# Adaptive-norm attention and gated feed-forward on one core: a prologue rearranged around a half-size scale block, and the output weights loaded by rows of 128 partitions

## The chip, the cores and the metric

One NeuronCore of a Trainium2 chip runs the whole block. The metric is the device time of one execution in microseconds (us). Durations of single instructions come from one profiled execution.

## The reference, cut to what matters

```
mod = (silu(c) @ w_mod).reshape(1, 6, 1, 1024)      # c: 1x1024, w_mod: 1024x6144
sa, ca, ga, sb, cb, gb = mod[:, 0..5]
h = layernorm(x) * (1 + ca) + sa                    # x: 2048x1024
q, k, v = split(h @ wqkv, 32 heads of 32)
pq, pk = phi(q), phi(k)     # phi(t) = (t + 1 if t > 0 else exp(t)) + 1e-6
kv = sum over tokens of pk^T v;   z = sum over tokens of pk
o = (pq @ kv) / (pq . z + 1e-6)                     # per head
x = x + ga * (o @ wo)
h = layernorm(x) * (1 + cb) + sb
x = x + gb * ((silu(h @ w_gate) * (h @ w_up)) @ w_down)   # 3584 wide
```

All inputs and the output are bf16.

## The kernel before, in words

The 2048 tokens are four blocks (`sc`, 0 to 3) of 512, each four tiles of 128. Attention needs kv and z over all tokens first: so for each block the program does K, then V (block 0: V, then K, then Q), and kv of the block before inside the next block's K. Then come Q of the other blocks, the output projection (`wo_tile`), and the feed-forward (`gate_up`, `down`), which is most of the time. A K, V or Q group is eight matmuls of 128x128x512 into one of four PSUM banks (`acc_a`, pool `pa`); other sums take a second pool of four (`acc_b`).

**What sets the order.** `mm` and `transpose` (L97, L100) keep TensorE in program order. `in_order` (L83) does the same for VectorE, ScalarE and GpSimd in the prologue (L474 to L529). Elsewhere the scheduler places instructions when it thinks them ready, by program order among ready ones; `tc.issue_after(x)` holds one back until `x`. All loads but two go through SP's queue. `hold_back` (L369) writes one element of a tile that a load will fill, after the latest phi, so that the load cannot start before that point.

**The prologue.** `c` is turned onto partitions by a small matmul and silu gives `scT`. `w_mod`'s columns 1024 to 2047 (`ca`, tiles `wca`, 2 MB) are loaded first, then `wv` with x tiles 2 and 3 between, `sa`'s block `wsa` and `wk`. `mod_rows(1, ...)` (L255) makes the `ca` row from `wca` with matmuls of 256 columns on four column groups, `mod_turn` (L262) turns it onto partitions. `hT` holds block 0's normalised tokens turned by TensorE (`pe_transpose_tile`, L217), `hs` the same times (1 + ca). V of block 0 uses `hs`, since the shift by `sa` is added to V's sums later; `mod_rows(0, ...)` makes `sa` during V, `modulate_all` (L413) then applies both to `hT` for K and Q. `sc_row`, silu(c) along the free axis on all partitions, comes from eight small matmuls (L485 to L489). `keep_warm` matmuls on zeros (`sel`) fill TensorE's waits.

**The other four rows of `mod`.** `mod_load(q, cols)` (L374) loads one row's block of `w_mod` turned, by two DMA transposes into two tiles of 4x1024; each `mod_step` (L384) multiplies one 128x1024 row set by `sc_row` on VectorE and sums it into one column. Row 2 (`ga`) is loaded at the end of block 0, row 3 in block 1, row 4 in block 3. `K_STEPS` and `V_STEPS` (L400) say how many steps go where. `ga_spread` (L403) brings `ga` along the free axis to all partitions by way of DRAM.

**wo.** In block 2, after the fourth K group, `wo` is loaded into two tiles [128, 4, 1024] (L550 to L556): eight DMAs, each to 32 partitions with four rows of 1024 on each. `wo_v` (L62) is `"(h g i e) n -> h g e i n"`. In block 3 each row is multiplied by `ga` on VectorE (L568 to L572). `ln1(sc)` (L242) gives block `sc` its `hT`: statistics, `xn` on ScalarE, and one DMA transpose per tile on SP (L239), then the modulation on VectorE. That of block 3 is made during block 2's late K groups and V.

**The fold.** After the last kv, `fold_wo(h, nb)` (L602) multiplies kv into `wo`: 16 matmuls of 32x32x512, each on a tile of the array of its own, into four `acc_b` banks, copied back over `wo` by ScalarE and VectorE. Four of these stand between Q groups.

Of the kernel before, what the change touches and what calls it, by code (L numbers as in the profile page):

```python
# [21 lines left out]
def kernel(  # L22
# [13 lines left out]
    nc = tc.nc  # L36
# [77 lines left out]
    c_sb = const.tile([DC, P], BF16, name="c_sb")  # L114

# [8 lines left out]
    for st in range(2):  # L124
        load_x(st, nc.sync)
# [3 lines left out]
    wca = [big("wme", [4, D]) for _ in range(2)]  # L129
# [6 lines left out]
    for j in range(DC):  # L136
        load_block(wca, wm_v, j, D, nc.scalar if j == 0 else nc.sync)
    for cc in range(DC):
        load_block(wv, wqkv_v, cc, 2 * D)
        if cc in (1, 4):  # L140
            load_x(2 + cc // 4, nc.sync)
# [26 lines left out]
    sc_row = const.tile([P, D], BF16, name="sc_row")  # L168
# [11 lines left out]
    sel = const.tile([P, HPC, P], BF16, name="sel")  # L180
# [17 lines left out]
    def bn(src, mv_out):  # L198
        stats = small.tile([P, NNB, nc.vector.BN_STATS_DIM], F32, name="stats")
        for i in range(NNB):  # L200
            nc.vector.bn_stats(out=stats[:, i, :], in_=src[:, i * NB:(i + 1) * NB])  # L201
        nc.vector.bn_aggr(out=mv_out, in_=stats[:])

    def normalise(dst, src, mean, rstd):
        nc.vector.tensor_scalar(out=dst, in0=src, scalar1=mean, scalar2=rstd, op0=ALU.subtract, op1=ALU.mult)

    def normalise_act(dst, src, mv, rstd):
        nmr = small.tile([P, 1], F32, name="nmr")
        last_nmr[0] = nc.gpsimd.tensor_scalar(out=nmr[:], in0=mv[:, 0, 0:1], scalar1=rstd[:, 0:1], scalar2=-1.0,  # L209
                                op0=ALU.mult, op1=ALU.mult)  # L210
        nc.scalar.activation(out=dst, in_=src, func=ACT.Identity, bias=nmr[:], scale=rstd[:, 0:1])  # L211
# [5 lines left out]
    def pe_transpose_tile(hT, xn, t):  # L217
        tp = acc_b("tp", (DC, P), BF16)
        for cc in range(DC):
            transpose(tp[:, cc, :], xn[:, cc * P:(cc + 1) * P])  # L220
        nc.vector.tensor_copy(out=hT[:, :, t * P:(t + 1) * P], in_=tp[:])
# [3 lines left out]
    def ln1_stats(sc, t):  # L225
        x_sb = x_tiles.pop(sc * STC + t)
        mv = small.tile([P, STC, 2], F32, name="mv")
        bn(x_sb, mv[:, 0, :])
        rstd = rstd_of(mv, 1)
        return sc, t, x_sb, mv, rstd  # L230

    def ln1_norm(sc, t, x_sb, mv, rstd, dve=False):
        xn = k2.tile([P, D], BF16, name="xn", bufs=4)
        if dve:
            normalise(xn[:], x_sb[:], mv[:, 0, 0:1], rstd[:, 0:1])
        else:
            normalise_act(xn[:], x_sb[:], mv, rstd)
        if sc > 0:
            last_load[0] = nc.sync.dma_start_transpose(hTs[sc][:, :, t * P:(t + 1) * P], xn[:])  # L239
        return xn  # L240
# [14 lines left out]
    def mod_rows(q, lo, hi, first=None):  # L255
        for j in range(lo, hi):
            if first is not None:
                mm(first, lhsT=wca[j // 4][:, j % 4, 0:P], rhs=scT[:, j:j + 1], start=False, stop=j == DC - 1)
            row_matvec(mod_ps[:, q * MW:(q + 1) * MW], sc32[:, j, :], (wsa, wca)[q][j // 4][:, j % 4, :],
                       q == 0 and j == 0, j == DC - 1)  # L260
# [4 lines left out]
    def scale_to(hs, hT, cc, lo, hi):  # L265
        nc.vector.tensor_scalar(out=hs[:, cc, lo:hi], in0=hT[:, cc, lo:hi], scalar1=ca0T[:, cc:cc + 1], scalar2=None,
                                op0=ALU.mult)

# [105 lines left out]
    def mod_load(q, cols, held=False):  # L374
        ts = [big("wmt", [DC // 2, D]) for _ in range(2)]
        if held:
            hold_back(ts)
        for h, t in enumerate(ts):
            lo = q * D + h * NB
            last = nc.sync.dma_start_transpose(t[:], w_mod[:, lo:lo + NB])  # L380
            mod_steps.extend((t[:, i, :], cols[:, 4 * h + i:4 * h + i + 1]) for i in range(DC // 2))
        return last
# [71 lines left out]
    nc.vector.memset(sel[:], 0.0)  # L454

    def keep_warm(acc, n):
        for _ in range(n):
            mm(acc[:], lhsT=sel[:, 0, :], rhs=sel[:], start=True, stop=True)

    def keep_warm_f32(acc, n):  # L460
        zeros = sel[:].rearrange("p h n -> p (h n)").bitcast(F32)
        for _ in range(n):
            mm(acc[:, 0:zeros.shape[1]], lhsT=zeros[:, 0:P], rhs=zeros, start=True, stop=True)

    accs = [acc_a() for _ in range(4)]
    spare = accs[3]
    keep_warm_f32(spare, 3)
    keep_warm(spare, 1)
# [5 lines left out]
    with in_order(nc.vector, nc.scalar, nc.gpsimd):  # L474
        mod_ps = acc_b("mod_ps")
        mm(mod_ps[:, 0:DC], lhsT=c_sb[:], rhs=ident[0:DC, 0:DC], start=True, stop=True)
        for g in range(4):
            mm(mod_ps[g * DH:(g + 1) * DH, MW:2 * MW], lhsT=ident[:, 0:DH], rhs=base_t[:, 0:MW], start=True, stop=False)
        nc.scalar.activation(out=scT[:], in_=mod_ps[:, 0:DC], func=ACT.Silu)
        xn0 = ln1_norm(*ln1_stats(0, 0))  # L480
        st1 = ln1_stats(0, 1)
        nc.vector.tensor_copy(out=sc32[:], in_=scT[:].unsqueeze(2).to_broadcast([P, DC, DH]))
        xn1 = ln1_norm(*st1, dve=True)
        keep_warm_f32(spare, 1)
        for h in range(2):  # L485
            for j in range(DC // 2):
                mm(accs[h][:, j * P:(j + 1) * P], lhsT=scT[:, 4 * h + j:4 * h + j + 1].to_broadcast([P, P]), rhs=ident[:],
                   start=True, stop=True)
            nc.scalar.copy(out=sc_row[:, h * NB:(h + 1) * NB], in_=accs[h][:])  # L489
        keep_warm(spare, 3)  # L490
        first = accs[2][:, 0:1]
        mm(first, lhsT=ident[:], rhs=base_t[:, 0:1], start=True, stop=False)
        mod_rows(1, 0, 3, first)
        pe_transpose_tile(hT, xn0, 0)
        pe_transpose_tile(hT, xn1, 1)
        mod_rows(1, 3, DC, first)
        keep_warm(spare, 1)
        nc.vector.tensor_scalar(out=hs[:, 0, 0:H], in0=hT[:, 0, 0:H], scalar1=first, scalar2=None, op0=ALU.mult)
        mod_turn(DC, 2 * DC)
        for cc in range(1, 4):  # L500
            scale_to(hs, hT, cc, 0, H)
        xn2 = ln1_norm(*ln1_stats(0, 2))
        for cc in range(4, DC):
            scale_to(hs, hT, cc, 0, H)
        st3 = ln1_stats(0, 3)
        gs = k_groups[0:4]
        v_mms(hs, gs, accs, 0, 6)
        pe_transpose_tile(hT, xn2, 2)
        for cc in range(DC):
            scale_to(hs, hT, cc, H, H + P)  # L510
        xn3 = ln1_norm(*st3)
        v_mms(hs, gs, accs, 6, DC)
        gs2, accs2 = k_groups[4:6], [acc_b("acc") for _ in range(2)]
        v_mms(hs, gs2[0:1], accs2[0:1])
        v_evac(0, gs, accs)
        pe_transpose_tile(hT, xn3, 3)
        for cc in range(DC):
            scale_to(hs, hT, cc, H + P, SCW)
        v_mms(hs, gs2[1:2], accs2[1:2])
        mod_rows(0, 0, DC)  # L520
        mod_turn(0, DC)
        nc.vector.tensor_copy(out=sca[:], in_=scr[:, :, :, 0])
        v_evac(0, gs2, accs2)
        for g in k_groups[6:8]:
            acc = acc_a()
            v_mms(hs, [g], [acc])
            v_evac(0, [g], [acc])
        modulate_all(hT, ca1T, saT)
# [4 lines left out]
    for h in range(2):  # L533
        with tc.issue_after(last_load[0].ins):
            nc.sync.dma_start(out=wq[h][:], in_=wqkv_v[:, 4 * h:4 * h + 4, 0:D])
# [5 lines left out]
    for sc in range(NSC):  # L541
        if sc > 0:
            k_phase(sc, 0, 2)
            kv_phase(sc - 1)
            k_phase(sc, 2, 3)
            if sc == 1:
                mod_load(3, sbT, True)
                mod_step(1)
            k_phase(sc, 3, 4)
            if sc == 2:  # L550
                wo = [big("wo", [4, D]) for _ in range(2)]
                hold_back(wo)
                for h in range(2):
                    for g in range(4):
                        with tc.issue_after(last_load[0].ins):
                            last_load[0] = nc.sync.dma_start(out=wo[h][g * DH:(g + 1) * DH, :, :], in_=wo_v[h, g])  # L556
            if sc == 3:
                mod_load(4, cbT, True)
            k_phase(sc, 4, 8)
        if sc == 0:  # L560
            k_phase(0, 0, 8)
# [24 lines left out]
        if sc == 0:  # L586
            with tc.issue_after(last_load[0].ins):
                last_load[0] = mod_load(2, gaT)

    q_phase(1, 0, 1, 2)  # L590
    q_phase(1, 1, 2)
# [10 lines left out]
    def fold_wo(h, nb):  # L602
        ns = slice(nb * NB, (nb + 1) * NB)
        ps = [acc_b("wf") for _ in range(4)]
        for i in range(HPC):
            for g in range(4):
                rs = slice(g * DH, (g + 1) * DH)
                mm(ps[g][i * DH:(i + 1) * DH, :], lhsT=KVT[rs, h, i * DH:(i + 1) * DH], rhs=wo[h][rs, i, ns],
                   start=True, stop=True)
        for g in range(4):  # L610
            (nc.scalar.copy if g % 2 == 0 else nc.vector.tensor_copy)(out=wo[h][:, g, ns], in_=ps[g][:])

    q_phase(1, 2, 5)
# [5 lines left out]
    den_sum(0, acc_a())  # L619
    fold_wo(0, 0)  # L620
    den_spread(0)
    q_phase(1, 6, 8)
    fold_wo(0, 1)
    q_phase(2, 0, 2)
    fold_wo(1, 0)
    q_phase(2, 2, 4)
    fold_wo(1, 1)
# [3 lines left out]
    def wo_tile(st):  # L631
# [10 lines left out]
        for nb in range(NNB):  # L642
            ns = slice(nb * NB, (nb + 1) * NB)
            a_ps = acc_b("a_ps")
            for hg in range(HG):
                mm(a_ps[:], lhsT=pq[:, hg, t * P:(t + 1) * P], rhs=wo[hg // 4][:, hg % 4, ns],
# [145 lines left out]
```

## Time and profile before

| | us |
|---|---|
| median of 3 runs | 829.96 (829.62 to 830.33) |
| the profiled execution | 830.19 |
| its span, first to last instruction | 828.4 |
| first V matmul (block 0) starts | 11.13 |
| first K matmul (block 0) starts | 27.60 |
| wo's loads issued | 94.7 to 97.9 |
| first K matmul of block 3 starts | 113.00 |
| the four folds start | 155.1, 159.1, 163.0, 166.9 |

A page of a profile gives busy time by engine, a picture of the span in 40 slices, DMA queues, the chain of work that ended last, and the costliest groups of instructions. PE is TensorE, DVE VectorE, ACT ScalarE, POOL GpSimd, SP SyncE; a q after an engine is its queue of DMA issues. In a group's line, `a<-b` is output and inputs by the program's names, and what follows is partitions x elements. A timeline's columns are start, duration, engine, line, operation and count. A window's columns are the stretch, its length, busy time and count of instructions of PE, PEld (weight loads), DVE, ACT and POOL, the granted clock, the busy share of the 16 DMA engines (which can pass 1, since packets overlap) and GB/s.

### The profile page before, as it was taken

How to read it: one execution, taken by the hardware profiler on the slowest of the kernel's cores; microseconds unless marked ns; L12 is line 12 of the kernel's file. 1: busy time of each engine (PE TensorE's matmuls, PEld its weight loads, DVE VectorE, ACT ScalarE, POOL GpSimd, SP SyncE). 2: the span in 40 equal slices, each digit the busy share in tenths (PEclk: the TensorE clock that was granted, in tenths of full speed). 3: DMA queues.
4: the chain of work that ended last, by engine and by line, in shares of the span. 5: the costliest groups of instructions: out<-in, count | busy, mean ns of one | idle time of the engine just before them, and what ended most of it. 6: DMA issues, size and time to landing. Idle time of an engine off the chain costs nothing.

```text
span 828.4 us, 11209 instructions
## 1 busy us (share of the span) xinstructions
PE 818.2 (99%) x4531; PEld 379.1 (46%) x4609; DVE 348.7 (42%) x680; ACT 168.1 (20%) x253; POOL 64.0 (8%) x165
## 2 busy tenths in 40 slices
PE   8999999999999999999999999999999999999998
PEld 4444444444444444444444444444444444444444
DVE  6868778886353344422222354222224432222222
ACT  3535343434111101101111010111111101111000
POOL 2101020120222002000000010000001100000000
PEclk9999999999999999999999999999999999999999
DMA  9968444139995836456342262753405529610011
GB/s 347 301 167 187 124 112 102 41 96 320 368 246 196 251 110 181 150 168 195 103 158 96 62 222 88 254 187 110 145 0 182 149 65 358 217 47 1 19 58 51
DMA packets 142212, 129.07 MB, mean 156 GB/s; under 512 B 58768, under 2 KB 120720, under 8 KB 141648
## 3 DMA queue, kind: packets, MB, share of 16 engines
q1 hardware_dynamic: 138208, 115.10, 46.3%
q0 software_dynamic: 3792, 12.98, 5.0%
q8 instruction: 36, 0.59, 0.3%
q10 hardware_dynamic: 160, 0.26, 0.1%
q14 instruction: 16, 0.13, 0.0%
HBM read 101.98 MB, written 12.72 MB: 138 GB/s over the span
## 4 chain that ended last, share of the span: by engine, by line
PE 97%; DMA 2%; issue 1%; DVE 0%; ACTq 0%; SPq 0%
PE acc L98 89%; PE a_ps L98 7%; DMA wv<-in_A_wqkv_dram 1%; PE kvp L98 1%; DMA wme<-in_w_mod_dram 0%; PE wf L98 0%; PE den L98 0%; PE mod_ps L98 0%; PE vb L98 0%; ACTq L126 0%; PE tp L101 0%; SPq L134 0%; DVE e L708 0%; DVE ob L711 0%
## 5 line engine op out<-in xcount | busy, mean ns | idle before, releaser
L98 PE MATMUL acc<-h2T,wgu 128*128 128x512 bf16 x1755 | 385.6, 379 | 1.9
L98 PEld LDWEIGHTS <-wgu 128*128 128x128 bf16 x1792 | 175.3, 98 | 211.3
L687 DVE TENSOR_TENSOR gu<-acc,e 128x512 bf16<-128x512 f32 x112 | 77.5, 692 | 289.9 <-PE acc L98 278.8
L98 PE MATMUL acc<-wd,gu 128*128 128x512 bf16 (+2 forms) x908 | 195.2, 372 | 0.9
L686 ACT ACTIVATE e<-acc 128x512 f32<-128x512 f32 x112 | 66.9, 597 | 374.8 <-PE acc L98 363.4
L98 PEld LDWEIGHTS <-gu 128*128 128x128 bf16 x924 | 89.3, 98 | 104.5
L708 DVE TENSOR_TENSOR e<-acc,gb_bc 128x512 f32<-128x512 f32 (+2 forms) x33 | 22.3, 675 | 131.7 <-PE acc L98 122.8
L98 PEld LDWEIGHTS <-hT 128*128 128x128 bf16 x448 | 43.6, 98 | 52.3
L98 PE MATMUL a_ps<-wo,pq 128*128 128x512 bf16 x250 | 56.9, 379 | 0.3
L98 PE MATMUL acc<-hT,wq 128*128 128x512 bf16 x250 | 55.9, 379 | 0.6 <-issue 0.5
L98 PE MATMUL acc<-wk,hT 128*128 128x512 bf16 x252 | 55.9, 379 | 0.4 <-issue 0.3
L273 ACT ACTIVATE eb<-acc 128x512 bf16<-128x512 f32 x64 | 37.6, 594 | 61.7 <-PE acc L98 57.3
L211 ACT ACTIVATE xn<-x,nmr,rstd 128x1024 bf16<-128x1024 f32 x16 | 19.8, 1240 | 126.2 <-POOL nmr L209 125.4
L98 PE MATMUL acc<-wv,hT 128*128 128x512 bf16 x186 | 41.6, 379 | 0.3
L98 PEld LDWEIGHTS <-pq 128*128 128x128 bf16 x256 | 25.1, 98 | 30.2
L655 POOL DMA_DIRECT2D x_scratch<-x x16 | 9.8, 615 | 373.5 <-DVE x L648 373.4
L98 PEld LDWEIGHTS <-wq 128*128 128x128 bf16 x256 | 24.6, 98 | 29.9 <-issue 1.1
L274 DVE TENSOR_SCALAR eb<-eb 128x512 bf16<-128x512 bf16 x64 | 18.3, 290 | 26.0 <-ACT eb L273 26.0
L648 DVE TENSOR_TENSOR x<-a_ps,x_sb 128x512 f32<-128x512 f32 x32 | 22.1, 691 | 8.6 <-PE a_ps L98 7.9
L195 POOL TENSOR_TENSOR rstd<-veps,neg_half 128x1 f32<-128x1 f32 x32 | 18.0, 561 | 99.5 <-DVE veps L193 87.0
L201 DVE BATCH_NORM_STATS2 stats<-x_sb 128x6 f32<-128x512 bf16 x32 | 20.9, 674 | 4.4 <-DMA x_sb<-in_A_x_dram 4.3
L711 DVE TENSOR_TENSOR ob<-e,x1r 128x512 bf16<-128x512 f32 (+2 forms) x33 | 22.3, 675 | 1.0
(99 smaller groups left out, 320.6 us busy)
## 6 DMA issues: line engine op xcount, KB each, us to landing
wgu<-in_B_w_gate_dram SPq DMA_DIRECT2D x28, 1024.0 KB, 6.4
wgu<-in_B_w_up_dram SPq DMA_DIRECT2D x28, 1024.0 KB, 7.9
x_sb<-in_A_x_dram SPq DMA_DIRECT2D x32, 256.0 KB, 5.3
x_scratch<-x POOLq DMA_DIRECT2D x16, 512.0 KB, 3.1
x1r<-x_scratch SPq DMA_DIRECT2D x31, 256.0 KB, 2.9
wd<-in_B_w_down_dram SPq DMA_DIRECT2D x7, 1024.0 KB, 6.7
rbc<-rden_scratch POOLq DMA_DIRECT2D x16, 256.0 KB, 8.1
out_dram<-ob SPq DMA_DIRECT2D x31, 128.0 KB, 1.7
```

The lines of the kernel that those rows point to most:

```text
L98: return tc.keep_in_program_order(nc.tensor.matmul(out, lhsT=lhsT, rhs=rhs, start=start, stop=stop))
L195: nc.gpsimd.tensor_tensor(out=rstd[:, 0:n], in0=veps[:, 0:n], in1=neg_half[:].to_broadcast([P, n]), op=ALU.pow)
L201: nc.vector.bn_stats(out=stats[:, i, :], in_=src[:, i * NB:(i + 1) * NB])
L211: nc.scalar.activation(out=dst, in_=src, func=ACT.Identity, bias=nmr[:], scale=rstd[:, 0:1])
L273: nc.scalar.activation(out=e[:], in_=acc, func=ACT.Exp)
L274: nc.vector.tensor_scalar(out=e[:], in0=e[:], scalar1=1.0, scalar2=PHI_EPS, op0=ALU.min, op1=ALU.add)
L648: nc.vector.tensor_tensor(out=x1[:, ns], in0=a_ps[:], in1=x_t[:, ns], op=ALU.add)
L655: nc.gpsimd.dma_start(out=x1_dram[st * P:(st + 1) * P, :], in_=x1[:])
L686: nc.scalar.activation(out=sg[:], in_=ps[0][:], func=ACT.Silu)
L687: gm = nc.vector.tensor_tensor(out=guT[sc][f // GPT][:, f % GPT, :], in0=ps[1][:], in1=sg[:], op=ALU.mult)
L708: nc.vector.tensor_tensor(out=yt, in0=y_ps, in1=gb_bc[:, ns], op=ALU.mult)
L711: nc.vector.tensor_tensor(out=ob, in0=yt, in1=x1r, op=ALU.add)
```

## The change

- **Scale block in halves.** `wca` is loaded as two column halves of 512 (`load_ca`), each four DMAs of two row chunks. The first half comes ahead of `wv`'s first four chunks, the second ahead of x tile 3 and the other four. The first half's columns are made by matmuls of one column (`ca_cols`), and the first four chunks of `hs` are scaled straight from PSUM; the second half still goes through rows and a turn (`ca_rows`). V's groups run first on chunks 0 to 3, then on 4 to 7.
- **x tile 2 earlier**, ahead of the weights; tile 1's normalisation is split between VectorE and ScalarE; `hT` is copied from PSUM by ScalarE.
- **Two key groups side by side.** K's first two groups of block 0 take each chunk of `wk` in turn (`k_mms(0, k_groups[0:2], pair)`); the modulation of `hT` is done in two halves of 256 tokens. In later blocks kv stands after the first K group, not the second.
- **sc_row** is silu of one loaded row, written to DRAM by GpSimd and read back to all partitions by SP behind `wq`.
- **Turned `w_mod` loads half a block later.** Row 2's second half moves to block 1, row 3's second half to block 2, ahead of `wo`.
- **wo** is loaded by eight DMAs, each to 128 partitions with one row of 1024 on each.
- **The fold** writes into tiles of its own (`wof`) in three batches of 5, 6 and 5 units, each unit four matmuls and one copy, with one or two `acc_a` banks beside the `acc_b` ones.

```diff
-    wca = [big("wme", [4, D]) for _ in range(2)]
+    wca = [big("wme", [DC, NB]) for _ in range(2)]
...
-    for j in range(DC):
-        load_block(wca, wm_v, j, D, nc.scalar if j == 0 else nc.sync)
-    for cc in range(DC):
+    def load_ca(h, eng0):
+        for k in range(4):
+            js = slice(2 * k, 2 * k + 2)
+            (eng0 if k == 0 else nc.sync).dma_start(out=wca[h][:, js, :], in_=wm_v[:, js, D + h * NB:D + (h + 1) * NB])
+
+    load_ca(0, nc.scalar)
+    nc.scalar.dma_start(out=sc_row[0:1, :], in_=c)
+    for cc in range(4):
         load_block(wv, wqkv_v, cc, 2 * D)
-        if cc in (1, 4):
-            load_x(2 + cc // 4, nc.sync)
+    load_ca(1, nc.sync)
+    load_x(3, nc.sync)
+    for cc in range(4, DC):
+        load_block(wv, wqkv_v, cc, 2 * D)
...
+        def ca_cols(k):
+            for i in range(4):
+                for j in (2 * k, 2 * k + 1):
+                    mm(cols[i], lhsT=wca[0][:, j, i * P:(i + 1) * P], rhs=scT[:, j:j + 1], start=False,
+                       stop=j == DC - 1 and i in (0, 3))
...
+        v_mms(hs, gs, accs, 0, 1)
+        turn_half(xn1, 1, 1)
...
+        v_mms(hs, gs, accs, 1, 3)
+        tp2 = turn_tile(xn2)
...
+        v_mms(hs, gs, accs, 3, 4)
+        ca_rows()
+        mod_turn(DC + 4, 2 * DC)
...
+        gs2, accs2 = k_groups[4:6], [acc_b("acc") for _ in range(2)]
+        v_mms(hs, gs2, accs2, 0, 4)
...
+        v_mms(hs, gs, accs, 4, DC)
...
-            k_phase(sc, 0, 2)
+            k_phase(sc, 0, 1)
             kv_phase(sc - 1)
-            k_phase(sc, 2, 3)
+            k_phase(sc, 1, 3)
             if sc == 1:
-                mod_load(3, sbT, True)
+                mod_load(2, gaT, (1,), True)
+                mod_load(3, sbT, (0,), True)
                 mod_step(1)
             k_phase(sc, 3, 4)
             if sc == 2:
+                last_load[0] = mod_load(3, sbT, (1,), True)
                 wo = [big("wo", [4, D]) for _ in range(2)]
                 hold_back(wo)
                 for h in range(2):
-                    for g in range(4):
+                    for i in range(HPC):
                         with tc.issue_after(last_load[0].ins):
-                            last_load[0] = nc.sync.dma_start(out=wo[h][g * DH:(g + 1) * DH, :, :], in_=wo_v[h, g])
+                            last_load[0] = nc.sync.dma_start(out=wo[h][:, i, :], in_=wo_v[h, :, :, i, :])
...
+    wof = [big("wof", [4, D]) for _ in range(2)]
+    fold_units = [(h, nb, g) for h in range(2) for nb in range(NNB) for g in range(4)]
...
+    def fold_wo(accs):
+        units = [(fold_units.pop(0), acc) for acc in accs]
         for i in range(HPC):
-            for g in range(4):
+            for (h, nb, g), acc in units:
                 rs = slice(g * DH, (g + 1) * DH)
...
+    fold_wo([acc_b("wf") for _ in range(3)] + [acc_a() for _ in range(2)])
...
+    q_phase(2, 0, 1)
+    fold_wo([acc_b("wf") for _ in range(4)] + [acc_a() for _ in range(2)])
+    q_phase(2, 1, 4)
+    fold_wo([acc_b("wf") for _ in range(4)] + [acc_a()])
```

## The prediction, made before the changed kernel was run

> **What bounds the kernel now.** I read the page's first, second and fourth parts, then the chain of waits in order of time, then the timeline around every place that the diff touches.
>
> ```profile
> span 828.4 us, 11209 instructions
> ...
> PE 818.2 (99%) x4531; PEld 379.1 (46%) x4609; DVE 348.7 (42%) x680; ACT 168.1 (20%) x253; POOL 64.0 (8%) x165
> ...
> q10 hardware_dynamic: 160, 0.26, 0.1%
> ...
> PE 97%; DMA 2%; issue 1%; DVE 0%; ACTq 0%; SPq 0%
> ```
>
> TensorE is the chain. From 27.6 us to the end its matmuls of 512 columns start 0.216 us apart and no gap is over 0.6 us, so a change gains only ahead of 27.6 us or in instructions removed, and loses wherever it makes TensorE wait. The q10 line comes back below. The chain of waits shows the only DMA in it:
>
> ```profile
> 1.33 3.80 DMA wme<-in_w_mod_dram
> 5.52 5.48 DMA wv<-in_A_wqkv_dram
> 11.02 6.37 DMA wv<-in_A_wqkv_dram
> ```
>
> The first 11 us go to 2.5 MB of loads ahead of the first V matmul (11.13 us). The second place to look at is block 2, where `wo` is loaded and the transposes of the next block's `hT` follow on the same queue. SP's timeline there, one tile's view, and the matmuls and VectorE work after it:
>
> ```profile
> 94.66 3.65 SPq L556 DMA_DIRECT2D wo<-in_A_wo_dram  x8
> 101.72 7.08 SPq L239 DMA_TRANSPOSE hT<-xn  x4
> ```
> ```profile
> L556 SPq DMA_DIRECT2D wo<-in_A_wo_dram x8: 332/430/431, 94.7 to 97.9; - x8
> ...
> DMA to landing us min/median/max: 3.9/5.9/7.6
> ```
> ```profile
> 111.02 2.76 DVE L214 TENSOR_SCALAR hT<-hT,sca 128x512 bf16<-128x512 bf16 x8
> ```
> ```profile
> 113.00 3.62 PE L98 MATMUL acc<-wk,hT 128*128 128x512 bf16 x16
> ```
>
> The fourth transpose lands at 110.89 us (its completion count in the trace), the eight modulations run 111.02 to 113.78, and K of block 3 starts at 113.00. Its last chunk is needed at 113.00 + 7 x 0.216 = 114.5, so the slack of this chain is 0.7 us. What delays `hT` of block 3 by more stalls TensorE one for one; nothing stands ahead of K in its program order. Last, the DMA rate in two stretches of 2 us, the first in `wo`, the second in the prologue's 128-partition loads (last column GB/s):
>
> ```profile
> 102.00:104.00 2.00, 2.00 (x11) 0.94 (x10) 1.79 (x6) 2.00 (x4) 0.29 (x2) 1.00 1.07 246
> ```
> ```profile
> 18.00:20.00 2.00, 2.00 (x11) 0.88 (x9) 1.31 (x8) 2.00 (x4) 1.47 (x34) 1.00 1.05 390
> ```
>
> All 16 engines are busy in both. The packet records say why the rates differ: a 2,048-byte packet takes a median 84 ns in the prologue (10 to 20 us) and 155 ns in `wo` (95 to 104 us).
>
> [...] q10 carried the 8-row load of `c` and one 128-row load; 160 packets are 8 + 128 of data and 24 completion counts, 8 for the one and 16 for the other. So the 8-row load ran on 8 engines. [...] the first transpose was issued at 101.72, but its first 256-byte packet starts at 104.07, when the last `wo` packets are ending (104.9). [...]
>
> **The change part by part.**
>
> *wo loads (L552-556).* Removed: eight loads of 32 partitions x 4 rows. Added: eight of 128 partitions x 1 row, the same 2 MB and 1,024 packets. But the source view `wo_v[h, :, :, i, :]` has dimensions g (4, step 128 rows), e (32, step 1 row) and columns: g and e don't merge, so its slowest dimension is 4. [...] Four engines then carry 1,024 / 4 = 256 packets each, against 64 each on 16 before. Low bound of a packet: 84 ns, 21.5 us in all. High bound: 155 ns, 39.7 us[...]. I take 120 ns, the middle: 30.7 us.
>
> Timing: everything before is shifted by the prologue's gain, 1.2 us (below). Block 2's fourth K group is done at 93.2 (94.4 before). New there is one `w_mod` transpose (the half moved from block 1) ahead of `wo`: 4.2 us of SP time (that form's median issue). wo is issued from 97.5, its packets start 0.95 us later as before, behind the transpose's: 99.0. They end at 99 + 30.7 = 129.7. The four `hT` transposes queue behind on those four engines: 64 packets of 18 ns each per transpose and engine, 4.6 us; landing about 134.7; one modulation 0.35 and its start 0.15: K of block 3 at 135.2. It is planned for 113.0 - 1.2 = 111.8. **Stall 23.4 us** (14.2 at 84 ns, 32.7 at 155). What is moved past: the hT transposes, and three x loads (L636, not needed until about 172 us). SP's own eight-semaphore rotation (100 to 109 in the trace) makes the transposes wait for the first four `wo` loads as well, inside the same time.
>
> *Clock after the stall.* [...] I take 1.0.
>
> *Prologue.* Loads ahead of the first V matmul fall from 11 pieces of 256 KB to 8 (three of x, four of half a scale block, one of `wv`). Landings were 0.675 us apart: the 8th came at 8.75 us. The half-block pieces are 1 KB packets, 46 ns in the trace's `wgu` loads, against 42 per KB: four pieces cost 0.3 more, so `wv` lands near 9.05, and V starts near 9.2, 1.9 us earlier. Added on TensorE ahead of K: the second half's rows (32 matmuls of 128 columns, about 0.6), four more transposes (0.27), and a wait for that half, which lands near 14.3 while TensorE gets there at 13.5 (0.8). Taken away: stalls of about 0.5. V, 64 x 0.216 = 13.8, both late transposes 1.06, rows of `sa` 1.0, added in order, end at 26.4 against 27.6. VectorE has 8 us of work in that stretch of 16 and hides. Side by side, K's first two groups end at 26.4 + 3.45 = 29.85 against 31.05; `wk`'s last piece (28.68 before, 0.6 later now) lands at 29.3, used at 29.4. **-1.2** (between 0 and the DMA limit, -1.9).
>
> *Fold.* 64 matmuls of 32x32 in three batches instead of four. Before:
>
> ```profile
> L98 PE MATMUL wf<-wo,kvs x64: 384/384/385, 155.1 to 167.0; 32*32 32x512 bf16 x64
> ```
>
> Each batch of 16 uses 16 different tiles of the array, which start 3.4 ns apart: 0.46 us from the last wide matmul's end to the next one's start, 1.84 in four. Batches of 5, 6 and 5 units bring one row group twice, so every column step has two matmuls on one tile. If the queue stays in order behind the second, a batch takes 4 x 0.23 + 0.38 = 1.3, three 3.9: +2.1. If each tile waits alone, about 0.67 each: +0.2. I take **+2.0**[...]. Its five or six copies (0.59 and 0.68 us) lie beside 3.5 us or more of wide matmuls on two engines.
>
> *The rest at nothing.* kv one group earlier: v's last copy ends about 0.7 us after its matmuls, a K group covers 1.73. `sc_row` by way of DRAM: one 256 KB load behind `wq`, which lands near 38.3, needed at 40.2. `wof`: two tiles more while `wo` still lives, when `wv`, `wk` and v are dead.
>
> **Sum.** The profiled execution took 830.19, span 828.4 and 1.8 around it, 0.2 above the median of 829.96. -1.2 + 2.0 + 23.4 + 1.0 = +25.2, so about 855.
>
> **The rivals.** *R1: wo runs on 16 engines*[...]. For it: nothing in this trace shows a 4-row outer dimension. Against it: the 8-row load. Then wo takes 2 MB at 390 GB/s, 5.4 us, ends near 104.4, the transposes wait on their inputs as now, and K isn't late. Time 829.96 - 1.2 + 0.2 to 2.0: 829 to 831, **829.4 if the fold's tiles wait alone**, so not slower. It decides when wo ends before about 106.
> *R2: four engines, but the transposes reach the queue ahead of wo.* For it: the program orders SP by readiness, not by the text (an L636 load stands before wo now). Against it: the first transpose is ready 7 us after wo is. About 831.
> The ends of the forecast itself[...] are no rivals but its range.
>
> **How the numbers follow.** Forecast 0.75, its own range 844 to 865; R1 0.20; R2 0.05. A measurement here tells 0.2%, 1.7 us, from no change. Slower: 0.75, and 0.05 of the rivals where the fold costs its full price and the prologue gains little. Faster: 0.03 of R1. Same: 0.17. The range reaches to R1: 829 to 865.
>
> **What would show it.** Forecast right: wo's time to landing grows from 5.9 us towards 10 or more with about 60 GB/s moved, hT's four transposes land after 125 us, and TensorE has one gap of 14 to 33 us before K of block 3. First V matmul near 9.2, K near 26.4, each fold batch near 1.3 us. Wrong: no gap before that K, and wo's packets at 84 ns on all engines.

## The result, and the profile after

The change costs 2.5%: 850.8 us (median of 4 runs, 850.28 to 851.89) against 829.8 us for the kernel before (median of 4, 829.62 to 830.33), a ratio of 1.0254 with a 95% interval of 1.0236 to 1.0272. The prediction had about 855 and slower. The profiled execution took 851.21 us with a span of 849.4.

The page's first lines, and the group that carries block 3's first K matmul:

```profile
span 849.4 us, 11327 instructions
...
PE 827.4 (97%) x4623; PEld 380.1 (45%) x4623; DVE 346.4 (41%) x685; ACT 173.8 (20%) x261; POOL 65.3 (8%) x167
...
PEclk9999987999999999999999999999999999999999
...
L98 PE MATMUL acc<-wk,hT 128*128 128x512 bf16 x256 | 58.3, 387 | 17.3 <-DVE hT L224 17.2
```

TensorE is busy 9.2 us longer, the span is 21.0 longer: most of the loss is idle time. The last line says which: 17.2 us ahead of a K matmul, ended by VectorE's modulation of `hT`. The clock picture dips in slices 6 and 7 (106 to 149 us), so part of the longer busy time is slow time. TensorE and then VectorE there (start, duration, engine, line, operation, count, idle time before it and what ended it):

```profile
107.63 6.85 PE L98 MATMUL acc<-wv,hT 128*128 128x512 bf16 x31
131.71 3.59 PE L98 MATMUL acc<-wk,hT 128*128 128x512 bf16 x8 [17.23 <-DVE hT L224]
```
```profile
131.24 2.67 DVE L224 TENSOR_SCALAR hT<-hT,sca 128x512 bf16<-128x512 bf16 x8 [19.02 <-DMA hT<-xn]
```

VectorE had been waiting too, for a DMA, so the modulation is only the last link. SP's timeline shows the DMA's own queue, and two windows its rate (last two columns: busy share of the 16 engines, GB/s):

```profile
95.88 4.07 SPq L392 DMA_TRANSPOSE wmt<-in_w_mod_dram  x1
100.13 13.64 SPq L607 DMA_DIRECT2D wo<-in_A_wo_dram  x8
113.88 12.98 SPq L247 DMA_TRANSPOSE hT<-xn  x3
```
```profile
104.00:106.00 2.00, 2.00 (x11) 0.94 (x10) 1.93 (x8) 1.50 (x2) 0.91 (x3) 1.00 0.25 96
110.00:112.00 2.00, 2.00 (x11) 0.93 (x10) 2.00 (x3) 0.81 (x2) 0.00 (x0) 1.00 0.27 102
```

A busy share of 0.25 is that of four engines of 16 at work. In the trace each `wo` load has five completion counts (16 in the kernel before): one 0.4 us after the end of its issue and four later on, for the first load at 101.26 and at 105.89 to 106.61. Its 2,048-byte packets take a median 84 ns. They run from 101.6 to 125.6 us. The four transposes land at 126.6, 127.6, 128.7 and 131.1, and K of block 3 starts at 131.71.

The ledger, from the starts of the same matmuls in both traces:

| | before | after | what it adds |
|---|---|---|---|
| K of block 0 starts | 27.60 | 28.59 | +1.0 |
| K of block 2 starts | 84.11 | 85.44 | +0.3 |
| gap ahead of K of block 3 | none | 17.4 | +17.4 |
| from K of block 3 to the output projection's first matmul | 59.47 | 61.86 | +2.4: halved clock 2.2, fold 0.2 |
| the output projection's first matmul | 172.47 | 193.57 | sum +21.1 |

The clock record is halved from 119.5 to 136.6 us: the first eight K matmuls after the gap start 0.426 us apart, and kv takes 0.49 longer (8 x 0.21 + 0.49 = 2.2).

The prologue gained nothing. TensorE's first 12 us (`acc<-gb_bc` are the f32 matmuls on zeros of `keep_warm`, the one-column ones are `ca_cols`):

```profile
4.81 2.06 PE L98 MATMUL acc<-gb_bc 128*128 128x512 f32 x2
6.65 0.24 PE L98 MATMUL col<-scT,wme 128*128 128x1 bf16 x2
6.75 0.30 PE L98 MATMUL mod_ps<-scT,wme 128*128 128x1 bf16 x6
6.91 2.91 PE L98 MATMUL acc<-gb_bc 128*128 128x512 f32 x4
...
11.89 1.04 PE L98 MATMUL acc<-wv,hs 128*128 128x512 bf16 x4
```

The loads landed as predicted (`ca`'s half pieces at 6.5, 7.06, 7.75 and 8.46, the first of `wv` at 9.12), but V starts at 11.89. The second filler, four records, takes 2.91 us at the halved clock and stands in TensorE's program order ahead of the second pair of column chunks. The clock became full at 10.29; in the kernel before at 4.67.

The fold's first batch of five units (the last eight of its twenty matmuls, and the wide ones behind them; the group of five is one matmul at 176.12 and four from 176.28 on):

```profile
176.11 0.39 PE L98 MATMUL wf<-wo,kvs 32*32 32x512 bf16 x3
176.12 0.59 PE L98 MATMUL acc<-wo,kvs 32*32 32x512 bf16 x5
176.64 5.35 PE L98 MATMUL acc<-hT,wq 128*128 128x512 bf16 x24
```

### The profile page after: what moved, and what is told of

It is laid out like the page before. It is cut to its first block, busy times and chain, and to the rows that moved or that the text cites. A ratio compares the mean times of both kernels' runs of the same rounds, so it can differ in the third digit from the quotient of the medians.

```text
span 849.4 us, 11327 instructions
## 1 busy us (share of the span) xinstructions
PE 827.4 (97%) x4623; PEld 380.1 (45%) x4623; DVE 346.4 (41%) x685; ACT 173.8 (20%) x261; POOL 65.3 (8%) x167
## 4 chain that ended last, share of the span: by engine, by line
PE 97%; SPq 1%; DMA 0%; DVE 0%; issue 0%; ACT 0%; DVEq 0%
PE acc L98 89%; PE a_ps L98 7%; SPq L247 1%; PE kvp L98 1%; DMA hT<-xn 0%; PE mod_ps L98 0%; PE tp L101 0%; PE den L98 0%; PE wf L98 0%; PE vb L98 0%; ACT v L321 0%; SPq L691 0%; DVE gb_bc L466 0%; DVE hT L224 0%; DVE e L763 0%
## 5 line engine op out<-in xcount | busy, mean ns | idle before, releaser
L763 DVE TENSOR_TENSOR e<-acc,gb_bc 128x512 f32<-128x512 f32 (+2 forms) x33 | 22.3, 676 | 131.6 <-PE acc L98 128.7
L98 PE MATMUL acc<-wk,hT 128*128 128x512 bf16 x256 | 58.3, 387 | 17.3 <-DVE hT L224 17.2
L98 PE MATMUL a_ps<-wof,pq 128*128 128x512 bf16 x256 | 57.4, 379 | 0.0
L98 PEld LDWEIGHTS <-wq 128*128 128x128 bf16 x256 | 24.6, 98 | 30.7 <-issue 1.7
L221 ACT ACTIVATE xn<-x_sb,nmr,rstd 128x1024 bf16<-128x1024 bf16 (+1 forms) x17 | 19.6, 1163 | 14.3 <-POOL nmr L216 14.2
```

The lines of the kernel that those rows point to most:

```text
L98: return tc.keep_in_program_order(nc.tensor.matmul(out, lhsT=lhsT, rhs=rhs, start=start, stop=stop))
L221: nc.scalar.activation(out=dst[:, ws], in_=src[:, ws], func=ACT.Identity, bias=nmr[:], scale=rstd[:, 0:1])
L763: nc.vector.tensor_tensor(out=yt, in0=y_ps, in1=gb_bc[:, ns], op=ALU.mult)
```

## The experiments

The theory: `wo` on four engines, with `hT`'s transposes behind it on the same queue, makes the gap and the halved clock after it (19.6 of 21.1 us). The rival: the loss comes of the new order in block 2 (a turned `w_mod` load ahead of `wo`, kv one group earlier) or of the tiles of 128 partitions. The first four kernels separate these. Each experiment's kernel has its number; 1, 3 and 4 start from the changed kernel, 2 from the kernel before. Ratios are to runs of the kernel before that were made beside them: medians 829.97 us for 1 to 4, 830.14 for 5 to 8, 830.28 for 9 and 10.

**1. wo as before, the rest of the change kept.**

```diff
-                    for i in range(HPC):
+                    for g in range(4):
...
-                            last_load[0] = nc.sync.dma_start(out=wo[h][:, i, :], in_=wo_v[h, :, :, i, :])
+                            last_load[0] = nc.sync.dma_start(out=wo[h][g * DH:(g + 1) * DH, :, :], in_=wo_v[h, g])
```

> The changed kernel with wo loaded as before: eight transfers of 32 partitions. Theory (four engines for the wo loads): their 256 packets on each of four engines are gone, the loads take 9.3 us as before, starting behind the moved w_mod transpose at about 101.6 us and ending near 111; the four hT transposes end near 116, some 2 us after K of block 3 is due (114.3), so a stall of 2.4 us is left, no halved clock: 829.8 + 1.3 (prologue and up to block 3) + 2.4 + 0.1 = 833.6. Rival (the w_mod transpose moved ahead of wo causes the stall, and the shape of wo's loads does not matter): 849 to 851, as the changed kernel.

Measured 833.38 us, ratio to before 1.0046 (1.0029 to 1.0063). That undoes 17.4 of 21.0 us. What is left shows in TensorE's timeline:

```profile
113.87 2.65 PE L98 MATMUL acc<-wk,hT 128*128 128x512 bf16 x8 [1.53 <-DVE hT L224]
116.45 1.22 PE L98 MATMUL kvp<-v,pk 128*32 128x64 bf16 x128
117.83 0.81 PE L98 MATMUL acc<-wk,hT 128*128 128x512 bf16 x3 [0.16 <-issue]
119.63 2.75 PE L98 MATMUL acc<-wk,hT 128*128 128x512 bf16 x12 [0.98 <-issue]
```

K of block 3 still waits 1.5 us for `hT`, and its eight matmuls are paced by VectorE (0.323 us apart, not 0.216: 0.75 in all). The wait of about 1.1 us at 119.63, with no releaser, I had not expected; it comes back below. In this execution the clock was full at 5.71, V of block 0 began at 9.80 and K at 26.50, close to the 9.2 and 26.4 of the prediction.

**2. The wo loads alone, put into the kernel before.** The diff of 1 turned round, on L554 to L556.

> The kernel before with nothing changed but wo's loads: eight transfers of 128 partitions from a source whose outermost dimension is 4. Theory: wo runs on four engines from 95.6 us at 84 ns a packet, about 23 us, to 118.6; the hT transposes land near 124; K of block 3 starts at 124.6 and not 113.0, a stall of 11.6, and 2.2 us for the halved clock: 829.8 + 13.8 = 843.6. Rival (the moved transpose causes the stall): 829.8, no change.

Measured 844.53 us, ratio 1.0175 (1.0155 to 1.0196). SP, and TensorE with the gap:

```profile
94.28 12.77 SPq L556 DMA_DIRECT2D wo<-in_A_wo_dram  x8
107.16 8.11 SPq L239 DMA_TRANSPOSE hT<-xn  x1
```
```profile
125.47 4.74 PE L98 MATMUL acc<-wk,hT 128*128 128x512 bf16 x13 [12.69 <-DVE hT L214]
```

The loads alone make the gap. It is 4.5 us shorter than in the changed kernel. No turned `w_mod` load stands ahead of `wo` here: its packets start at 95.8 us and not at 101.6, while block 2's K starts 1.7 us earlier.

**3. Eight loads of 128 partitions that do run on 16 engines.** Each reads 128 consecutive rows. The output projection then multiplies by `wo`'s rows in another order than the reference's; the work is the same.

```diff
+    wo_rows = A_wo.rearrange("(h i p) n -> h i p n", h=2, p=P)
...
-                            last_load[0] = nc.sync.dma_start(out=wo[h][:, i, :], in_=wo_v[h, :, :, i, :])
+                            last_load[0] = nc.sync.dma_start(out=wo[h][:, i, :], in_=wo_rows[h, i])
```

> The changed kernel, but each wo transfer reads 128 rows that lie one after another in DRAM, so that the source's outermost dimension is 128 and not 4; the destination, its 128 partitions, the bytes and the count of packets stay. It puts wo's rows in another order, so the output projection uses permuted rows: its time alone is of interest. Theory: 16 engines, 5.4 us for wo, ending near 107.5, hT in time, no stall: 829.8 + 1.4 = 831.2. Rival 1 (128 partitions per transfer are slow in themselves): 849 to 851. Rival 2 (moved transpose): 849 to 851.

Measured 831.41 us (15 runs, 830.56 to 833.39), ratio 1.0022 (1.0015 to 1.003). One tile's view:

```profile
L608 SPq DMA_DIRECT2D wo<-in_A_wo_dram x8: 376/430/442, 98.3 to 101.6; - x8
...
DMA to landing us min/median/max: 2.7/4.6/5.4
```

The tile's shape and its 128 partitions are those of the change; only the source pattern differs. An issue takes SP 0.43 us (0.99 with the four-row dimension) and the loads are over within 5.4 us of issue. So it is the source pattern with the four-row outer dimension that costs.

**4. Four engines kept, but wo issued behind hT's transposes.** The load block moves unchanged from block 2's fourth K group to behind `ln1(3)`.

```diff
-                wo = [big("wo", [4, D]) for _ in range(2)]
-                hold_back(wo)
...
             ln1(sc + 1, [last_on[nc.vector.engine]] * 2 + [i.ins for i in last_phi[2:4]] if sc == 0 else [last_phi[-5].ins] * STC)
+        if sc == 2:
+            wo = [big("wo", [4, D]) for _ in range(2)]
+            hold_back(wo)
...
```

> The changed kernel with wo's loads left on four engines but issued behind the hT transposes of block 3. Theory (the loss is the transposes queueing behind wo on these four engines, not wo's own lateness): wo takes the same 21 to 24 us, from about 110 to 133 us, needed by VectorE near 131 and by TensorE at 156, so no stall of TensorE: 829.8 + 1.4 = 831.2, 832 if the scaling of wo by ga is late. Rival (slow loads cost wherever they stand, since wo itself is waited for): 840 or more, with a gap before the folds.

Measured 830.44 us (13 runs, 829.42 to 832.73), ratio 1.0009 (1.0001 to 1.0017).

```profile
109.50 1.24 SPq L247 DMA_TRANSPOSE hT<-xn  x1
110.83 14.86 SPq L621 DMA_DIRECT2D wo<-in_A_wo_dram  x8
```
```profile
104.65 9.88 PE L98 MATMUL acc<-wv,hT 128*128 128x512 bf16 x44
114.36 1.99 PE L98 MATMUL acc<-wk,hT 128*128 128x512 bf16 x8
```

The same slow transfer costs nothing that shows on TensorE: no gap stands ahead of K of block 3, and the time is within 0.2% of the kernel before. VectorE waits 1.1 us for `wo`, beside TensorE's work. In the changed kernel the loads hurt by what stood behind them on their queue: 17.4 us there, no gap here.

**5. The rest of kernel 1: the turned w_mod loads back where they were.** Added to the edit of kernel 1:

```diff
-                mod_load(2, gaT, (1,), True)
-                mod_load(3, sbT, (0,), True)
+                mod_load(3, sbT, held=True)
...
-                last_load[0] = mod_load(3, sbT, (1,), True)
...
-                last_load[0] = mod_load(2, gaT, (0,))
+                last_load[0] = mod_load(2, gaT)
```

> As e1 (wo by 32 partitions), and the turned w_mod loads put back to where they were before (row 2 whole in block 0, row 3 whole in block 1), so that no transpose stands ahead of wo in block 2. Theory (the moved half, 4 us of SP and engine time ahead of wo, is what is left of the stall in e1): K of block 3 starts on time, 2.5 us less than e1: about 830.9, between 829.5 and 832 by when the clock rises in the prologue. Rival (the rest of the stall comes from something else in block 2): 833.4 as e1.

Measured 830.91 us (12 runs, 829.27 to 834.06), ratio 1.0011 (1.0002 to 1.0019). The wait ahead of K of block 3 is gone (28.88 us from block 2's K to block 3's, the same as before's 28.89): the moved load had cost kernel 1 its delay. The profiled execution was the slowest, and has a wait without a releaser again, now in block 1. The clock is halved after it, from 60.96 to 64.38 us, and both together cost 4 us (block 1's K to block 2's takes 33.0 us, in kernel 4 28.9):

```profile
57.78 1.03 PE L98 MATMUL acc<-wk,hT 128*128 128x512 bf16 x4 [0.16 <-issue]
61.19 3.15 PE L98 MATMUL acc<-wk,hT 128*128 128x512 bf16 x7 [2.39 <-issue]
```

**6 and 7. The prologue's fillers.** Both start from kernel 4. The first moves one filler ahead of the two small matmuls that open the columns' sums; the second leaves out the fillers between the column matmuls.

```diff
+        keep_warm(NB)
         mm(cols[0], lhsT=ident[:], rhs=base_t[:, 0:1], start=True, stop=False)
         mm(mod_ps[:, DC:DC + 3], lhsT=ident[:], rhs=base_t[:, 0:3], start=True, stop=False)
-        keep_warm(NB)
```
```diff
         ca_cols(0)
-        keep_warm(NB, 2 * P)
         ca_cols(1)
...
         ca_cols(2)
-        keep_warm(P)
...
         ca_cols(3)
-        keep_warm(P)
```

> As e4, with one filler matmul pair of the prologue moved ahead of the two small matmuls that wait for ScalarE, so that TensorE is not idle for the 0.4 us near 4.5 us. Theory[...]: the clock is full by 8.3 us in every run, the first V matmul between 9.8 and 10.9, no run as late as e4's profiled one (12.1): median 829.6, spread of the runs under 1.6 us where e4's was 3.3. Rival (when the clock rises is chance, whatever stands there): median 830.4 and the spread of e4.

> As e4, without the filler matmuls between the column matmuls of the scale block. Theory (fillers on zeros cost TensorE twice their time while the clock is halved and set when V starts, but without them the clock is still halved when V starts): first V matmul near 9.4, its matmuls 0.43 us apart[...], K of block 0 at 27.6 to 29.3: 829.8 to 832. Rival (the fillers only stand in the way): V at 9.4 at full clock, K at 25.9: 828.5.

The first gave 830.51 us, ratio 1.0004 (0.9995 to 1.0012). Eleven of its thirteen runs lie between 829.65 and 831.16, two far off (1,537 and 3,110 us) for a cause that I don't know; the ratio is of the eleven. So the spread fell from 3.3 us to 1.5 as expected, though kernel 4 ran on another chip; that the idle time had held the clock back (it was full at 5.98 us here, at 11.0 in kernel 4, one execution each) is not shown. The median did not fall, and the profile says why: V of block 0 starts at 9.81 and K at 26.51, 1.1 us ahead of the kernel before, and the gain is given back. K of block 3 starts at 112.18, 0.8 ahead, with its last chunks already paced by VectorE (0.323 us apart); from there to the output projection it takes 60.42 us against 59.47. The pacing is 0.4 of that, a short stop after kv (in the table under 10) 0.2, the fold 0.2; the rest stays open. The first matmul of the projection is at 172.6 against 172.47.

The second gave 830.3 us (829.46 to 832.12), ratio 1.0005 (0.9997 to 1.0013), inside what was expected. Its clock was full from 4.54 to 7.95, then halved again until 11.36; V started at 9.59 and K at 27.14. Without fillers nothing at the halved clock stands in V's way, but V's own first matmuls run at it.

**8. wo by 32 partitions, behind hT.** Kernel 6 with the loads of kernel 1 (the diff of 1).

> As p1, with wo loaded by 32 partitions behind the hT transposes: no stall in block 3, wo landed near 121 us, the prologue's gain kept: 829.3 by the theory, the candidate for a kernel that is not slower than either. If the clock's rise is chance, 830.4.

Measured 837.58 us, ratio 1.009 (1.0077 to 1.0104): a miss by 8 us. The place that was free for the load on four engines was not free for this one on 16:

```profile
114.43 1.22 PE L98 MATMUL kvp<-v,pk 128*32 128x64 bf16 x128
115.81 0.81 PE L98 MATMUL acc<-wk,hT 128*128 128x512 bf16 x3 [0.16 <-issue]
121.86 3.33 PE L98 MATMUL acc<-wk,hT 128*128 128x512 bf16 x8 [5.25 <-issue]
```

TensorE stands still for 5.4 us, the profile shows nothing that it waits for, and the clock is halved from 121.39 to 124.80. The page's DMA part names a small queue:

```profile
q8 instruction: 36, 0.59, 0.3%
```

36 packets of 16 KB of the kind that the page calls `instruction`: I read them as instructions on their way to an engine. By their count they fit TensorE: its 4,623 matmuls and 4,623 weight loads make 257 for each packet, and in the feed-forward one starts every 27.5 us on average, while 128 matmuls 0.216 us apart, with 128 weight loads, take 27.6. In kernel 6 one starts at 114.27, just ahead of kv, whose 256 short instructions (128 matmuls 8 ns apart, each with its weight load) follow each other far faster than K's, whose matmuls are 0.216 us apart. In this kernel that packet started only at 119.04, and TensorE went on 2.8 us later. My new theory: the fetch queues behind `wo`'s packets on its DMA engine.

**9 and 10. Two tests of that.** Kernel 9 holds the loads of kernel 8 back to block 3's fourth K group; kernel 10 leaves them where they are but reads consecutive rows, at full rate (rows of `wo` in another order, as in kernel 3).

```diff
             if sc == 3:
+                wo = [big("wo", [4, D]) for _ in range(2)]
+                hold_back(wo)
...
                 mod_load(4, cbT, held=True)
...
-        if sc == 2:
-            wo = [big("wo", [4, D]) for _ in range(2)]
-            hold_back(wo)
...
```

> As p4_wo32_behind (the wo loads by 32 partitions behind hT's transposes, which left TensorE without work for 5.41 us after kv in block 3), but with the loads held back until the fourth K group of block 3. Theory (TensorE's own 16 KB instruction fetch, due right after kv's 256 short instructions, queued behind wo's packets on all 16 engines): by the fourth K group that fetch has long landed and the next ones have slack, so no gap over 1 us in block 3, first a_ps about 172.6, median 829.5 to 830.5. Rival (the 32-partition loads hurt by themselves, through VectorE's wait for wo or the modulation): the loss stays, 835 or more, since wo is needed at the same place and now comes later.

> As p4_wo32_behind, but each wo transfer reads 128 consecutive rows, one per partition (so the output projection multiplies by wo's rows in another order than the reference). All 16 engines at 84 ns a packet: wo's packets run from about 108.4 for 5.4 us and end near 113.8, ahead of TensorE's fetch after kv (114.3 without traffic). Theory of the fetch: gap after kv in block 3 under 1 us, median 829.5 to 831. Rival (any wo load in that place costs, whatever its length): about 837.

Measured 839.9 us, ratio 1.0114 (1.0098 to 1.0131), and 837.0 us, ratio 1.0079 (1.0064 to 1.0094). By their times both went to the rival. By their traces neither supports it. Kernel 9:

```profile
117.94 11.38 PE L98 MATMUL acc<-wk,hT 128*128 128x512 bf16 x52 [0.21 <-issue]
...
163.29 0.61 PE L98 MATMUL wf<-wo,kvs 32*32 32x512 bf16 x3 [6.99 <-DVE kvs L673]
```

The gap in K is gone, and the fetch starts at 115.75. A new one of 7.15 us stands ahead of the fold: the later load pushed eight steps of `mod` (9.2 us of VectorE, 151.6 to 160.8) and half of the scaling of `wo` (2.5 us) between `kvs` and its copy, where kernel 6 had done both by 150.1; the clock is halved from 158.74 to 168.98. That is VectorE's time, but not the wait that the rival names, and I had not foreseen it. Kernel 10 has a gap of 3.60 us in K, and the clock is halved from 119.42 to 126.25. I expected its packets to end at 113.8; they share the engines with `hT`'s transposes, three x loads and `ga_spread`, and the 2,048-byte packets, the x loads' among them, run at 135 to 199 a microsecond from 115 us on, with 82 more in the one that begins at 118. The fetch starts at 118.19. I misjudged when the load ends; the fetch was late again, by 5.5 us after the K group, and the stop came with it.

Six kernels in order of the fetch's delay after the start of the block's first K group (a gap is the step between two matmuls less 0.216 us):

| kernel | K starts | fetch starts | delay | TensorE goes on | gap |
|---|---|---|---|---|---|
| 6 | 112.18 | 114.27 | 2.1 | 116.62 | 0.2 |
| 9 | 113.25 | 115.75 | 2.5 | 117.94 | 0.4 |
| 1 | 113.87 | 117.22 | 3.3 | 119.63 | 1.1 |
| 5 (block 1) | 54.57 | 58.6 | 4.0 | 61.19 | 2.6 |
| 10 | 112.69 | 118.19 | 5.5 | 120.68 | 3.6 |
| 8 | 111.93 | 119.04 | 7.1 | 121.86 | 5.4 |

The gap grows with the delay. In all six TensorE resumes 2.2 to 2.8 us after the fetch starts, 1.2 to 1.6 us after the packet ends, and in block 3 always behind the third or fourth K matmul that the trace has after kv. Kernels 3 and 4 have a step of 0.40 and 0.34 us at that place, 2.4 us after their packet's start. Kernel 7, with 16 TensorE instructions fewer ahead, has none, though its packet starts 2.9 us after the K group. That fits an engine that comes to a fixed count of instructions before the next packet is in. It is agreement in time: no run delayed the fetch by itself, so the mechanism is supported, not isolated. What the late packets queue behind is less clear still: the trace doesn't say on which DMA engine a packet ran, and it is not `wo` alone. In kernel 1 `wo` is over by 108.4 us and x loads run up to 117.6; in block 1 of kernel 5 there is no `wo`.

No version is measurably faster than the kernel before; kernels 6 and 7 come level with it.

## Why the prediction was right, and where not

**Right, and shown by kernels 2, 3 and 4.** wo runs on four engines: a busy share of 0.25, and four completion counts a load behind the one that follows its issue. Ahead of the run this was my estimate from a slowest dimension of 4, next to the 8-row load with its 8 counts. Kernel 3, with 128 consecutive rows a load, shows that the source pattern makes the difference; other patterns were not tried. `hT`'s transposes, issued behind it on the same queue, land at 126.6 to 131.1, after its end at 125.6, and TensorE stops once, ahead of K of block 3, inside the 14 to 33 us given. R1 and R2 are out: the pattern was not cut over 16 engines, and the transposes were issued after `wo`.

**The stall, 17.4 against 23.4: the packet was mis-sized.** I took 120 ns, the middle; it is 84, the low bound. The 32-partition loads do take longer (155 ns a packet in the kernel before, 162 in kernel 8), these don't. Why was not shown, and that these might take 155 as well was my estimate. With 84 ns the load should take 21.5 us; it took 24.0. It began at 101.6 and not at 99.0, so it ended at 125.6 and not at 129.7. The transposes landed 5.5 us later, not 5.0. And the start the stall is counted from came 2.5 later than planned, since the prologue gained nothing: 23.4 - 4.1 + 0.5 - 2.5 = 17.3. (The prediction's upper end, 32.7, is a slip: 39.7 - 30.7 = 9.0 on top of 23.4 is 32.4.)

**The halved clock, 2.2 against 1.0.** The place was right. The 1.0 was my estimate, which no trace of the kernel before shows. The clock stayed halved for 4.9 us after TensorE resumed (131.71 to 136.58), 3.6 in kernel 2 and 2.9 in kernel 8, so it is no fixed time after a gap. What agrees is the length of the halved stretches: 17.07 us here, 13.65 in kernel 2, 3.41 in kernel 8, which is five, four and one times 3.41. Here the stretch began at 119.51, 5.2 us into the gap. Counted from there in steps of 3.41, TensorE resumed in the fourth step (129.75 to 133.17), and the clock was full only at the end of the fifth.

**The prologue, +1.0 against -1.2: the step that failed.** The data came when I said. I had priced `keep_warm` at nothing, as a filler of waits, and the clock as full. A filler stands in program order: at the halved clock one of four records takes 2.91 us, in kernel 1 with the clock full 1.54. The clock's rise differs from one execution to the next: 5.7 in kernel 1, 10.3 in the changed kernel, 11.0 in kernel 4, with K of block 0 at 26.5, 28.6 and 28.8. Kernel 6, with one filler moved, was full at 5.98 and its runs spread half as far. Even at its best the gain is not worth 1.2: in kernel 6, 1.1 us ahead at K of block 0, VectorE's `hT` of block 3 takes 0.4 back and the stop after kv 0.2, and my sum had neither.

**The fold, about +0.2 against +2.0: the wrong branch.** I had both prices and took "in order", which no trace had shown. The second matmuls on a tile of the array waited alone: the fifth unit's four start from 176.28 on, 0.016 us apart, while sixteen on other tiles, twelve of them behind the first of these four in program order, had all started by 176.12. Three batches of 0.58 to 0.60 us (the first 176.06 to 176.64) stand against four of 0.37; with the 0.09 ahead of it a batch comes to 0.68, and I had 0.67 for that branch.

That the sum came within 4 us is in part luck, since the errors partly cancel: -6.0 in the stall, +1.2 in the clock, +2.2 in the prologue, -1.8 in the fold and +0.3 of small gaps between blocks 0 and 2 that I did not list make -4.1. The sum of the prediction, 830.19 + 25.2 = 855.4, less 4.1 is 851.3; the profiled execution took 851.21.

## What to carry to other kernels

Before a load is given a new shape, look at the slowest dimension of its source pattern: here a 4 there left four of 16 DMA engines at work (a busy share of 0.25 against 1.07), and what was lost was the time of everything behind it on the queue, so the same load behind the urgent transfers cost next to nothing (kernel 4, ratio 1.0009). Price every instruction that stands in an engine's program order, fillers too, at the clock the trace grants it, and ask which later engine takes a gain back. When a busy engine stops with no releaser named, look among the DMA queues for packets of the kind `instruction`.

## What the runs showed of the hardware

- **TensorE stood still where a packet of instructions came late.** A 16 KB packet (36 of them on q8, kind `instruction`; by their count they fit TensorE) started up to 7.1 us after the K group instead of 2.1, while other loads ran, and TensorE stood still for up to 5.4 us, until 1.2 to 1.6 us after the packet's end. In kernel 6 it started at 114.27 in the middle of `wo` on four engines, and the stop was 0.2 us. This is agreement in time in six kernels, no more.
- **Small tiles of the array waited one by one.** Twenty matmuls of 32x32x512 on 16 tiles took 0.58 us, not twice a single one's 0.38: twelve started ahead of one that stands before them in program order and whose tile was busy.
- **When the clock became full was not fixed.** In ten profiled executions with the new prologue it first did between 4.5 and 11.0 us, with the same instructions or nearly the same; in kernel 7 it fell back at 7.95.
- **The halved clock came in whole stretches of 3.41 us, once inside a stop of 2.6 us.** Apart from those at a program's end, seven stretches in the traces last one, two, three, four or five times 3.41 us (17.07 in the changed kernel, 6.83 in kernel 10, 10.24 in kernel 9). The one in kernel 5 began inside that stop; the stop of 1.1 us in kernel 1 had none.
